# Issuing the last V tile whole and ahead of the FFN weights, with a semaphore for each weight, in a one-core decode block

## The chip, the cores and the metric

The kernel runs on one core of a Trainium2 chip. The metric is the device time of one execution in microseconds. Of the kernel before, three runs gave 677.16, 677.44 and 677.42 us (median 677.42). Every run told here was of the state "fast". The profiled execution is a little shorter by its own account (the span of the profile of before is 675.6 us), so spans are compared with spans and times with times.

## The reference

One decoding step of a transformer block: layer norm, attention of 2 x 32 heads over a cache of 8192 keys, output projection, residual, layer norm, a gated FFN, residual. Batch 2, width 512, head width 128, FFN width 1376, all bfloat16.

```python
x = A_x                                             # 2 x 1 x 512
h = x + _A_ref(_layernorm(x), A_k_cache, A_v_cache, A_wq, A_wo)
h2 = h + _B_ref(_layernorm(h), B_W_gate, B_W_up, B_W_down)
# _A_ref: q = x @ wq;  p = softmax(q k^T / sqrt(128));  (p v) @ wo
# _B_ref: (relu(x @ W_gate) * (x @ W_up)) @ W_down
```

The two caches are 268 MB, so almost all the work is to stream them through once.

## The kernel before

The 64 heads are worked off as 32 tiles p of two heads. For each p one K tile and one V tile of 4096 KB are loaded into four slots (K of even p in slot 0, V of odd p in slot 3). VectorE (DVE) computes three quarters of the scores of a K tile, TensorE (PE) the rest; ScalarE (ACT) takes the exponentials; PE multiplies them with V (128 matmuls, "the PV"). The FFN weights go to slot 0 once K30 is done with. All loads are issued by one queue, in program order:

```python
                def load_v(p, parts=None):
                    sv = (2 * p + 1) % 4
                    if p >= 2:
                        sp.wait(t_pv[p - 2])          # the slot's last reader
                    ...                               # (cut) whole, or in `parts` with sem_vl each
                # in the loop over p, after the scores of tile p:
                    if p + 2 < NP:
                        sp.wait(*t_kfree[p])
                        t_k[p + 2] = load(s, slot[s][:], kv(A_k_cache, p + 2))
                    ...                               # (cut)
                    elif p == NP - 2:                 # p = 30
                        sp.wait(*t_kfree[p])          # slot 0 free: DVE has read K30
                        for k, w in enumerate((B_W_up, B_W_gate)):
                            nc.sync.dma_start(..., w...).then_inc(sem_w, 16)
                        load_v(p + 1, vparts)         # V31 in four parts
                        nc.sync.dma_start(..., B_W_down[0:10 * 128]...).then_inc(sem_wd, 16)
```

The tail behind the loop, in PE's order (cut):

```python
                pv(NP - 2)
                t_O[3] = normalize(3, 24, 31, t_batch[3], False)   # DVE, queued behind the last scores
                pe.wait(t_O[3])
                o_proj(range(HM, 30), 0, 2)
                o_proj(range(30, 32), 0, 1)
                normalize(4, 31, 32, z_sum(4, 31, 32), True)
                pv(NP - 1)                                         # "the last PV"
                ...                                                # scale, o_proj, residual, mean
                pe.wait((sem_w, 32), t_d)
                t_u = ffn_in(Sp[1], wup, 0, FC)                    # up: 44 matmuls
                t_g = (ffn_in(Op[1], wgt, 0, FH), ffn_in(Wp, wgt, FH, FC))   # gate: 24 + 20
                ...
                pe.wait((sem_wd, 32))                              # down: 44 matmuls, then the result
```

The softmax here doesn't subtract the row's maximum and nothing guards it: scores larger than these inputs give would overflow.

## Time and profile before

| | before |
|---|---|
| time, median of 3 | 677.42 us |
| profiled span | 675.6 us |
| DMA | 281.97 MB, 417 GB/s mean |
| busy share of PE, DVE, ACT | 44%, 73%, 30% |

The page of the kernel before: the DMA rows of the 40 slices (tenths busy, and GB/s), and the chain that ended last, by engine.

```profile
DMA  9999999999999999999999999999999999999993
GB/s 373 433 434 370 430 426 432 427 430 428 434 427 430 430 434 429 432 434 427 424 428 430 431 432 434 429 432 430 426 429 428 431 428 433 428 430 392 418 411 117
...
DMA 73%; DVE 24%; PE 1%; issue 1%; SPq 0%; DVEq 0%
```

The DMA engines are busy until the last slice (16.9 us). A change to the order of the last loads can only move that last slice and a little before it.

The timeline of before, from 636 us to the end. Columns: start, duration, engine, line, operation, out<-in, count, and in brackets the idle time before it and what ended it. SPq lines are loads being issued.

```profile
638.40 0.33 SPq L428 DMA_DIRECT2D slot<-in_B_W_up_dram  x1
...
639.26 2.04 SPq L353 DMA_DIRECT2D slot<-in_A_v_cache_dram  x4
...
641.34 0.44 SPq L432 DMA_DIRECT2D slot<-in_B_W_down_dram  x1
...
658.96 1.23 PE L309 MATMUL W<-O_sb,X 128*128 128x2 bf16 x32 [6.68 <-DVE O_sb L297]
...
660.47 2.27 PE L334 MATMUL O<-e,slot 128*128 128x2 bf16 x80
...
664.30 1.44 PE L334 MATMUL O<-e,slot 128*128 128x2 bf16 x48 [1.55 <-DMA slot<-in_A_v_cache_dram]
...
667.36 1.53 PE L473 MATMUL S<-d_b,slot 128*128 128x2 bf16 x44 [0.35 <-DVE d_b L458]
...
670.19 1.47 PE L515 MATMUL O<-hd,slot 128*128 128x2 bf16 x40
```

V31 is issued only at 639.26, behind W_up and W_gate, since the queue first waits for slot 0. The last PV does 80 of its matmuls and then stands 1.55 us until another part of V31 is there. This is the one DMA wait of the tail's PE work.

The landings of before, from the view of DMA issues between 625 and 676 us (size of one, time from issue to landing). An issue's start plus this time is its landing.

```profile
slot<-in_A_v_cache_dram SPq DMA_DIRECT2D x1, 1536.0 KB, 21.5
slot<-in_B_W_up_dram SPq DMA_DIRECT2D x1, 1376.0 KB, 9.8
slot<-in_B_W_gate_dram SPq DMA_DIRECT2D x1, 1376.0 KB, 16.4
slot<-in_A_v_cache_dram SPq DMA_DIRECT2D x1, 1280.0 KB, 24.1
slot<-in_B_W_down_dram SPq DMA_DIRECT2D x1, 1280.0 KB, 26.9
```

The V31 part of 1280 KB was the third issued, at 640.20 by the chain of waits, so it landed at 664.25, which is the end of the PE wait. W_down landed at 641.34 + 26.9 = 668.2, before PE asks for it at 670.19.

### The profile page before, as it was taken

To read this page: it belongs to the slowest core of one execution; us is meant where nothing else is said; L and a number is where in the kernel's file an instruction comes from. 1 tells how busy PE (TensorE), PEld (TensorE's weight loads), DVE (VectorE), ACT (ScalarE), POOL (GpSimd) and SP (SyncE) were. 2 spreads that over 40 slices of the span, in tenths; PEclk is the share of its full clock that TensorE was granted. 3 is DMA by queue.
4 is the path that set the end of the run, shared out by engine and by line. 5 is a ranking of instruction groups with operands and counts; after the bars stand their busy time and mean duration, and the time that the engine had idled before them with its cause. 6 is when DMAs were issued, how large, how long until landed. Compare 5 with 4: busy or idle time off the path is not lost.

```text
span 675.6 us, 14430 instructions
## 1 busy us (share of the span) xinstructions
PE 294.0 (44%) x6596; PEld 266.2 (39%) x6596; DVE 493.6 (73%) x428; ACT 202.0 (30%) x523; POOL 1.7 (0%) x11
## 2 busy tenths in 40 slices
PE   2552254344445424443533444353344644334446
PEld 2442244333434423443433444343344534334335
DVE  1774577788777768877767887776788767778891
ACT  0630322233333223333312333331233332223330
POOL 1000000000000000000000000000000000000000
PEclk9955655566655566556556556555556555556555
DMA  9999999999999999999999999999999999999993
GB/s 373 433 434 370 430 426 432 427 430 428 434 427 430 430 434 429 432 434 427 424 428 430 431 432 434 429 432 430 426 429 428 431 428 433 428 430 392 418 411 117
DMA packets 15936, 281.97 MB, mean 417 GB/s; under 512 B 1442, under 2 KB 6916, under 8 KB 7044
## 3 DMA queue, kind: packets, MB, share of 16 engines
q1 hardware_dynamic: 15872, 281.06, 97.9%
q8 instruction: 51, 0.84, 0.5%
q14 instruction: 9, 0.07, 0.0%
q10 hardware_dynamic: 4, 0.00, 0.0%
HBM read 281.05 MB, written 0.00 MB: 416 GB/s over the span
## 4 chain that ended last, share of the span: by engine, by line
DMA 73%; DVE 24%; PE 1%; issue 1%; SPq 0%; DVEq 0%
DMA slot<-in_A_k_cache_dram 69%; DVE prod L366 15%; DVE tb L374 5%; DMA slot<-in_A_v_cache_dram 4%; DVE prod L374 3%; DVE scores L381 1%; PE S L473 0%; PE O L515 0%; PE O L334 0%; SPq L353 0%; SPq L135 0%; SPq L428 0%; PE W L473 0%; PE O L473 0%; PE W L309 0%
## 5 line engine op out<-in xcount | busy, mean ns | idle before, releaser
L366 DVE TENSOR_TENSOR prod<-slot,q_b 128x6144 bf16<-128x6144 bf16 x64 | 214.9, 3358 | 132.3 <-DMA slot<-in_A_k_cache_dram 131.1
L334 PE MATMUL O<-e,slot 128*128 128x2 bf16 x4096 | 118.7, 165 | 239.2 <-DMA slot<-in_A_v_cache_dram 119.8
L334 PEld LDWEIGHTS O<-e,slot 128*128 128x128 bf16 x4096 | 114.6, 104 | 243.5 <-ACT e L267 122.0
L397 ACT ACTIVATE kT<-T 128x1024 bf16<-128x1024 bf16 x128 | 126.5, 1022 | 170.6 <-PE T L391 169.7
L391 PE MATMUL T<-ident,slot 128*128 128x128 bf16 x1024 | 122.6, 306 | 77.5 <-DMA slot<-in_A_k_cache_dram 75.2
L374 DVE TENSOR_TENSOR tb<-prod 128x3072 bf16<-128x3072 bf16 (+1 forms) x128 | 148.2, 1158 | 4.4
L391 PEld LDWEIGHTS T<-ident,slot 128*128 128x128 bf16 x1024 | 99.7, 141 | 80.5 <-DMA slot<-in_A_k_cache_dram 78.2
L267 ACT ACTIVATE e<-scores 64x48 bf16<-64x48 f32 x128 | 32.8, 256 | 253.2 <-DVE scores L381 251.6
L374 DVE TENSOR_TENSOR prod<-tb 128x1536 bf16<-128x1536 bf16 (+1 forms) x128 | 84.2, 658 | 4.4
L259 PE MATMUL S<-qT,kT 128*128 128x2 bf16 x1024 | 48.2, 168 | 39.0 <-ACT kT L397 37.8
L259 PEld LDWEIGHTS S<-qT,kT 128*128 128x128 bf16 x1024 | 40.8, 107 | 57.6 <-ACT kT L397 57.6
L381 DVE TENSOR_REDUCE scores<-prod 128x48 f32<-128x384 bf16 x64 | 35.4, 553 | 2.2
L267 ACT ACTIVATION_READ_ACCUMULATOR e<-scores 64x1 f32 x128 | 23.6, 185 | 0.0
L267 ACT ACTIVATE e<-S 64x32 bf16<-64x32 f32 x64 | 12.9, 202 | 15.0 <-PE S L259 14.2
L267 ACT ACTIVATION_READ_ACCUMULATOR e<-S 64x1 f32 x64 | 12.9, 201 | 0.7
L212 DVE CAST qT<-W 128x64 bf16<-128x64 f32 x1 | 0.2, 225 | 12.0 <-PE W L207 12.0
L241 ACT ACTIVATE q_b<-O 128x512 bf16<-128x512 f32 x8 | 4.3, 595 | 15.6 <-PE O L236 15.6
L309 PE MATMUL W<-O_sb,X 128*128 128x2 bf16 (+1 forms) x136 | 5.0, 172 | 7.0 <-DVE O_sb L297 7.0
L309 PEld LDWEIGHTS W<-O_sb,X 128*128 128x128 bf16 x136 | 4.8, 118 | 7.2 <-DVE O_sb L297 7.2
L207 PE MATMUL W<-xlT,X 128*128 128x2 bf16 x128 | 3.6, 165 | 8.6 <-DMA X<-in_A_wq_dram 8.6
L207 PEld LDWEIGHTS W<-xlT,X 128*128 128x128 bf16 x128 | 3.5, 104 | 8.7 <-DMA X<-in_A_wq_dram 8.7
L285 DVE TENSOR_REDUCE zr<-O 128x16 f32<-128x48 f32 (+1 forms) x4 | 0.8, 204 | 8.3 <-PE O L277 8.3
(58 smaller groups left out, 39.3 us busy)
## 6 DMA issues: line engine op xcount, KB each, us to landing
slot<-in_A_k_cache_dram SPq DMA_DIRECT2D x32, 4096.0 KB, 27.8
slot<-in_A_v_cache_dram SPq DMA_DIRECT2D x31, 4096.0 KB, 32.2
X<-in_A_wq_dram SPq DMA_DIRECT2D x1, 4096.0 KB, 12.4
X<-in_A_wo_dram SPq DMA_DIRECT2D x1, 4096.0 KB, 49.1
slot<-in_A_v_cache_dram SPq DMA_DIRECT2D x1, 1536.0 KB, 21.5
slot<-in_B_W_up_dram SPq DMA_DIRECT2D x1, 1376.0 KB, 9.8
slot<-in_B_W_gate_dram SPq DMA_DIRECT2D x1, 1376.0 KB, 16.4
slot<-in_A_v_cache_dram SPq DMA_DIRECT2D x1, 1280.0 KB, 24.1
```

The lines of the kernel that those rows point to most:

```text
L207: i = nc.tensor.matmul(Wp[:, h * B:(h + 1) * B], lhsT=wq[:, c, h * Dh:(h + 1) * Dh], rhs=lT[:, c * B:(c + 1) * B], start=(c == 0), stop=(c ...
L241: t_cp[m] = act.run(nc.scalar.activation(out=q_b[:, m * 512:(m + 1) * 512], in_=Op[m % 2][:], func=ACT.Copy))
L259: i = nc.tensor.matmul(Sp[p % 2][:, 2 * jj:2 * jj + 2], lhsT=kT[n % 3][:, k * 128:(k + 1) * 128], rhs=qT[:, 2 * p:2 * p + 2], start=True, ...
L267: t = act.run(nc.scalar.activation(out=e_t[p % 2][q, j0:j0 + nj, a], in_=src(q, a), func=ACT.Exp, scale=inv_sqrt_dh, accum_out=zs[q, 2 * p ...
L285: dve.run(nc.vector.tensor_reduce(out=zr[:, 2 * p0:2 * p1], in_=zbank(k)[:, 64:64 + n * (NCH + 1)].rearrange("p (n k) -> p n k", k=NCH + 1 ...
L309: i = nc.tensor.matmul(Wp[:, c * B + b0:c * B + b1], lhsT=wo_m[:, h, c, :], rhs=Ov[:, h // 2, h % 2, b0:b1], start=first[0], stop=last, sk ...
L334: i = nc.tensor.matmul(Op[k % 2][:, col:col + 2], lhsT=v_t[:, j, :], rhs=e_t[p % 2][:, j, :], start=(nmm == 0), stop=(nmm == J - 1))
L366: t_dm = dve.run(nc.vector.tensor_tensor(out=prod[:], in0=k_t[:, c * JC:(c + 1) * JC, :], in1=qv, op=ALU.mult))
L374: dve.run(nc.vector.tensor_tensor(out=o, in0=cur[:, :, 0:half], in1=cur[:, :, half:w], op=ALU.add))
L381: t_s = dve.run(nc.vector.tensor_reduce(out=sc[:], in_=cur, axis=AX.X, op=ALU.add))
L391: i = nc.tensor.transpose(Tp[n % 3][:, k * 128:(k + 1) * 128], k_t[:, j, :], ident[:])
L397: t_ev[n] = act.run(nc.scalar.activation(out=kT[n % 3][:], in_=Tp[n % 3][:], func=ACT.Copy))
```

## The change

The intent: V31 needs only slot 3, so it need not wait for slot 0. The order becomes K30, K31, V30, V31, W_up, W_gate, W_down. V31 goes whole. Since the weights are now the last to land, each gets its own semaphore, and W_down comes in two parts, so that PE can start on what is there.

```diff
-        sem_x, sem_wq, sem_wo, sem_w, sem_wd, sem_out = ...
-        sem_vl = [S(f"vl{i}") for i in range(4)]
+        sem_w = [S(f"w{i}") for i in range(2)]
+        sem_wd = [S(f"wd{i}") for i in range(3)]
 ... (cut)
                     elif p == NP - 2:
+                        load_v(p + 1)
                         sp.wait(*t_kfree[p])
                         for k, w in enumerate((B_W_up, B_W_gate)):
-                            nc.sync.dma_start(...).then_inc(sem_w, 16)
-                        load_v(p + 1, vparts)
-                        nc.sync.dma_start(... B_W_down[0:10 * 128] ...).then_inc(sem_wd, 16)
+                            nc.sync.dma_start(...).then_inc(sem_w[k], 16)
+                        for k, (r0, r1) in enumerate(WD_PARTS):      # (0, 6), (6, 10)
+                            nc.sync.dma_start(... B_W_down[r0 * 128:r1 * 128] ...).then_inc(sem_wd[k], 16)
 ... (cut)
-                pe.wait((sem_w, 32), t_d)
+                pe.wait(t_d)
+                pe.wait((sem_w[0], 16))
                 t_u = ffn_in(Sp[1], wup, 0, FC)
+                pe.wait((sem_w[1], 16))
                 t_g = (...)
 ... (cut)
-                pe.wait((sem_wd, 32))
+                pe.wait((sem_wd[2], 16))
                 for k, (f0, f1) in enumerate(((0, FH), (FH, FC))):
-                    pe.wait(t_hd[k])
+                    pe.wait(t_hd[k], (sem_wd[k], 16))
```

The arithmetic of PE, DVE and ACT, and its order on each engine, does not change.

More of the change, by code (lines that the diff above doesn't have):

```diff
@@ L68, in bass_sequential_preLN__gqa_block_cached__glu_gated_reglu__decode_kernel @@
     inv_sqrt_dh = 1.0 / math.sqrt(Dh)
-    BATCH = 8
+    WD_PARTS = ((0, 6), (6, 10))
     with ExitStack() as es:
@@ L87, in bass_sequential_preLN__gqa_block_cached__glu_gated_reglu__decode_kernel @@
         slot_cnt = [0] * 4
-        sem_x, sem_wq, sem_wo, sem_w, sem_wd, sem_out = S("x"), S("wq"), S("wo"), S("w"), S("wd"), S("out")
-        sem_vl = [S(f"vl{i}") for i in range(4)]
+        sem_x, sem_wq, sem_wo, sem_out = S("x"), S("wq"), S("wo"), S("out")
+        sem_w = [S(f"w{i}") for i in range(2)]
+        sem_wd = [S(f"wd{i}") for i in range(3)]
         slot = [sb(f"slot{i}", [128, SLOT], BF16) for i in range(4)]
@@ L156, in _ @@
                 t_v[1] = load(3, slot[3][:], kv(A_v_cache, 1))
-                nc.sync.dma_start(wd_last[:], B_W_down[F - FR:]).then_inc(sem_wd, 16)
+                nc.sync.dma_start(wd_last[:], B_W_down[F - FR:]).then_inc(sem_wd[2], 16)
                 pool.run(nc.gpsimd.memset(ident_f[:], 0.0))
@@ L317, in _ @@
                 t_batch = {}
-                vparts = ((0, 96, 128), (1, 0, 48), (2, 48, 88), (2, 88, 96))
                 W_AT = 24
@@ L325, in pv @@
                     col = 2 * (p - batches[k][0])
-                    parts = vparts if p == NP - 1 else (
-                        [(0, NCH * JC, J)] + [(1 + c, c * JC, (c + 1) * JC) for c in range(NCH)])
+                    parts = [(0, NCH * JC, J)] + [(1 + c, c * JC, (c + 1) * JC) for c in range(NCH)]
                     if p == batches[k][0] and k >= 2:
@@ L330, in pv @@
                     nmm = 0
-                    for ci, (ei, j0, j1) in enumerate(parts):
-                        pe.wait(t_exp[p][ei], (sem_vl[ci], 16) if p == NP - 1 else t_v[p])
+                    for ei, j0, j1 in parts:
+                        pe.wait(t_exp[p][ei], t_v[p])
                         for j in range(j0, j1):
@@ L342, in pv, with load_v @@
                             t_O[k] = normalize(k, *batches[k], t_batch[k], False)
-                def load_v(p, parts=None):
+                def load_v(p):
                     sv = (2 * p + 1) % 4
@@ L347, in load_v @@
                         sp.wait(t_pv[p - 2])
-                    if parts is None:
-                        t_v[p] = load(sv, slot[sv][:], kv(A_v_cache, p))
-                        return
-                    src = kv(A_v_cache, p)
-                    for ci, (_, j0, j1) in enumerate(parts):
-                        nc.sync.dma_start(
-                            slot[sv][:, j0 * Dh:j1 * Dh], src[:, j0 * Dh:j1 * Dh]).then_inc(sem_vl[ci], 16)
+                    t_v[p] = load(sv, slot[sv][:], kv(A_v_cache, p))
                 for p in range(NP):
@@ L429, in _ @@
                                 slot[0][:, k * DC * F:(k + 1) * DC * F],
-                                w.rearrange("(p c) n -> p (c n)", c=DC)).then_inc(sem_w, 16)
-                        load_v(p + 1, vparts)
-                        nc.sync.dma_start(
-                            slot[0][:, 2 * DC * F:2 * DC * F + 10 * D].rearrange("p (r n) -> p r n", n=D),
-                            B_W_down[0:10 * 128].rearrange("(r p) n -> p r n", p=128)).then_inc(sem_wd, 16)
+                                w.rearrange("(p c) n -> p (c n)", c=DC)).then_inc(sem_w[k], 16)
+                        for k, (r0, r1) in enumerate(WD_PARTS):
+                            nc.sync.dma_start(
+                                slot[0][:, 2 * DC * F + r0 * D:2 * DC * F + r1 * D].rearrange("p (r n) -> p r n", n=D),
+                                B_W_down[r0 * 128:r1 * 128].rearrange("(r p) n -> p r n", p=128)).then_inc(sem_wd[k], 16)
                 pv(NP - 2)
```

## The prediction

> What bounds the kernel now. The page says DMA moves 281.97 MB at a mean 417 GB/s, and its 40 slices show DMA at tenths 9 until the last slice. A 4096 KB K or V tile takes 9.7 us of that stream. The chain of waits is 73% DMA and 24% VectorE (DVE). So the body is bound by the bytes, which stay; only the tail can change.
>
> The tail, from the timeline and the chain (us from the start of the span):
> - 627.25 K30 has landed; DVE works without a gap on tiles 30 and 31 (K31 is there by 637) until 658.3; the exponentials end at 659.0.
> - TensorE (PE) stands idle from 652 to 658.95, waiting for O_sb, which DVE normalises only behind the last scores. Then 32 output-projection matmuls, the sum, and 80 of the last PV's matmuls (from 660.47, 2.27 us).
> - At 662.74 PE waits 1.55 us for a part of V31. V31 was issued in four parts at 639.3 to 640.8, behind W_up and W_gate, as the queue first waited for slot 0 (held until 638.4).
> - 664.30 the last 48 PV matmuls (1.44 us), 665.85 scale, projection, residual, mean; 667.36 up, gate, then down at 670.19, result written, end 675.6. W_down landed at 668.2 (26.9 us after issue) and ended no wait.
>
> What the change does.
> 1. V31 waits only for PV of 29, which ended at 625.5. It is issued about 13 us earlier, ahead of the weights. [...](K30, K31, V30, up, gate, V31, down land in issue order). V30 lands at 647.0, so V31 should land at about 656.7, or 658 with an instruction fetch in the way (one of 1.0 us was served at 653.1). PE asks for it at 660.47. The wait goes.
> 2. The same bytes now end with the weights. My estimate from the trace's rates: up lands at 661.3, gate 664.5, down part 1 at 666.7, part 2 at 668.1 (its 1 KB packets take 46 ns each, 22 GB/s per engine against 27 for the large ones, as before).
> 3. The last PV runs 128 matmuls in one go, 660.47 to 664.05. Everything behind it moves up 1.6 to 1.7 us: up asked for at 665.7, gate 667.2, down part 1 at 668.5, part 2 at 669.4. All have landed by then, with 1.3 to 4 us to spare, so the separate semaphores are worth about nothing.
> 4. Three DMA issues fewer and larger V packets: off the chain.
>
> So the gain is one wait, 1.6 us; not more, since the tail then hangs on DVE's 31 us from K30's landing and the chain behind it. Predicted 675.8 us, 0.2% less; 8 times in 10 between 674.4 and 677.2. Faster by over 2%: 1%; within 2%: 98%; slower by over 2%: 1%.
>
> What would show it: no PE wait on V before the last 48 PV matmuls; the last PV still starting near 660.5; V31 issued near 626; K30 and K31 landing unchanged; hardly any PE wait on the FFN weights; span near 674.0.
>
> What would make it wrong: the last landing moves to the back of the chain. The slower eight of the 16 DMA engines land 4.7 us behind the faster eight, one of them 1.8 us behind those; part 2 of W_down could land after 669.4 and give back up to 1 us. If V31's early issue delays K30 or K31, DVE shifts and the time grows by as much.

What the trace of before shows is the order of landings in the brackets, with last landings at 627.25, 636.95, 647.03, 648.25, 655.15, 657.49 to 664.93 (V31's parts) and 668.27 us. 677.4 less the one wait of 1.6 us is the predicted 675.8 us. V31's 656.7 is V30's 647.0 plus the 9.7 us of a tile.

The other figures of the DMA are from the same trace. The packets of 1 KB took 46 ns in the median, those of 32 KB 1.215 us, which are 22 and 27 GB/s; 16 times 27 is 432 GB/s, and the page's slices show up to 434. The packet of kind "instruction" at 653.08 took 1.00 us. Of the 16 landings of W_down eight came at 661.6 to 661.9, six at 666.4 to 666.9 and two at 668.0 and 668.3; of V31's third part eight at 657.2 to 657.5, seven at 662.4 to 662.9 and one at 664.25. That a landing stands for one engine is the reading, since the trace does not number the engines.

## The result

| | before | after |
|---|---|---|
| time, median of 4 each | 677.43 us (677.16 to 677.45) | 676.11 us (675.81 to 676.30) |
| profiled span | 675.6 us | 674.2 us |

The ratio is 0.9982, with a 95% interval of 0.9968 to 0.9996. Here and below a ratio is the mean time of one kernel's fast runs over that of the other's fast runs of the same rounds, so not quite the ratio of the medians quoted. The gain is 1.3 us, 0.2%.

The page of the changed kernel: the DMA row and the chain by engine.

```profile
DMA  9999999999999999999999999999999999999993
...
DMA 70%; DVE 27%; PE 2%; issue 1%; SPq 0%; DVEq 0%
```

The last V landing is off the chain, and the last two tiles' DVE work is on it.

The timeline of the changed kernel, from 624 us to the end, in the same columns.

```profile
625.32 0.33 SPq L136 DMA_DIRECT2D slot<-in_A_v_cache_dram  x1
...
638.14 0.33 SPq L422 DMA_DIRECT2D slot<-in_B_W_up_dram  x1
...
638.98 13.50 SPq L426 DMA_DIRECT2D slot<-in_B_W_down_dram  x2
...
658.69 1.23 PE L310 MATMUL W<-O_sb,X 128*128 128x2 bf16 x32 [6.68 <-DVE O_sb L298]
...
660.21 3.55 PE L333 MATMUL O<-e,slot 128*128 128x2 bf16 x128
...
665.29 0.50 PE L467 MATMUL S<-d_b,slot 128*128 128x2 bf16 x13 [0.26 <-DVE d_b L452]
...
666.22 1.18 PE L467 MATMUL S<-d_b,slot 128*128 128x2 bf16 x31 [0.42 <-issue]
...
668.70 1.48 PE L511 MATMUL O<-hd,slot 128*128 128x2 bf16 x40
```

V31 is issued 14 us earlier and the last PV runs its 128 matmuls in one go. But there is a new stop: after 13 matmuls of up PE stands for 0.42 us, and the profile gives "issue", that is, no wait on a semaphore that it can see. W_up had landed 4 us before. (The 13.50 us of the W_down line are the queue's time on its two issues; the second began at 639.46.)

The landings of the changed kernel, from the view of DMA issues between 625 and 676 us.

```profile
slot<-in_A_v_cache_dram SPq DMA_DIRECT2D x1, 4096.0 KB, 32.4
slot<-in_B_W_up_dram SPq DMA_DIRECT2D x1, 1376.0 KB, 22.9
slot<-in_B_W_gate_dram SPq DMA_DIRECT2D x1, 1376.0 KB, 25.8
slot<-in_B_W_down_dram SPq DMA_DIRECT2D x1, 768.0 KB, 27.3
slot<-in_B_W_down_dram SPq DMA_DIRECT2D x1, 512.0 KB, 28.2
```

V31 is there at 625.3 + 32.4 = 657.7, up at 661.0, gate at 664.3, down at 666.3 and 667.7. PE asks for them at 660.2, 665.3, 667.2, 668.7 and about 669.4. No landing ends a PE wait.

Each of these is the last of 16 landings, which come in two halves: of W_down's second part eight at 660.0 to 660.8 and eight at 665.9 to 667.7, two of these at 667.4 and 667.7. The faster half is done 6.8 us before the last landing. No run here tries to even this out.

Where the 1.4 us between the two profiled spans went, stretch by stretch (differences of the starts above):

| stretch | before | after | difference |
|---|---|---|---|
| up to the start of the last PV | 660.47 | 660.21 | -0.26 |
| the last PV | 5.27 | 3.55 | -1.72 |
| scale to start of up | 1.62 | 1.53 | -0.09 |
| up and gate, to start of down | 2.83 | 3.41 | +0.58 |
| down to the end | 5.4 | 5.5 | +0.1 |

The first line is not of the change: K30's landing starts it (DVE begins on K30 at 627.27 before and 627.01 after), and this lay between 627.0 and 627.6 in the traces of all runs. So the removed wait gave 1.7 us, and a third of that was lost again in the FFN. The stop costs more than its 0.42 us of idle time: idle time counts from the modelled end of the last matmul, and the starts on its two sides are 0.59 us apart, where they are 0.03 us apart in the rest of up.

### The profile page after: what moved, and what is told of

The parts are those of the page before. It is cut to its first block, busy times and chain, and to the rows that moved or that the text cites. A ratio compares the mean times of both kernels' runs of the same rounds, so it can differ in the third digit from the quotient of the medians.

```text
span 674.2 us, 14429 instructions
## 1 busy us (share of the span) xinstructions
PE 294.7 (44%) x6596; PEld 266.7 (40%) x6596; DVE 493.6 (73%) x428; ACT 202.2 (30%) x523; POOL 1.7 (0%) x11
## 4 chain that ended last, share of the span: by engine, by line
DMA 70%; DVE 27%; PE 2%; issue 1%; SPq 0%; DVEq 0%
DMA slot<-in_A_k_cache_dram 70%; DVE prod L359 16%; DVE tb L367 6%; DVE prod L367 4%; DVE scores L374 2%; PE O L333 1%; PE S L467 0%; PE W L310 0%; PE O L511 0%; SPq L136 0%; PE W L467 0%; PE O L467 0%; PE S L278 0%; SPq L152 0%; DVE O_sb L298 0%
```

## The experiments

The theory: the gain is V31's place in the queue and nothing else; the new stop in up is a refill of PE's instructions, which the wait on V31 had hidden before. The rivals: the gain comes from the separate semaphores, or from the whole transfer with fewer issues; and the stop is chance, or belongs to its place in the program.

The record behind the second part of the theory is in the trace of DMA packets. Besides the data queue it has packets of 16 KB on a queue of kind "instruction". The page of the changed kernel counts them:

```profile
q8 instruction: 51, 0.84, 0.5%
```

PE has 13,238 records (weight loads, matmuls and sequencer instructions) in this trace, 259.6 for each of the 51 packets; the other engines have 1,191 together. The page does not say which engine a packet is for. That these packets bring PE's instructions, 256 with each (13,238 is 51.7 times 256), was the assumption when the first expectations were written; the stops found in the tails of the runs below do lie 256 records apart (12,738, 12,994 and 13,250). Whether such a packet can stop PE is what the next runs test.

All experiments gave correct results. There were twelve runs of ten kernels, in three calls on three different chips; the runs of before beside them had medians of 677.10, 677.32 and 677.48 us. Numbers of different calls are compared by their distance from before.

### a_again and a_third: the changed kernel twice more

No edit. For a_again:

> The changed kernel once more, to narrow the interval and to see whether its new 0.4 us PE stop inside the W_up matmuls comes again. Both theories: 1.2 to 1.6 us faster than before (about 676.0). If the stop is an instruction refill of PE (a 256-instruction boundary), it stands at the same matmul, the 14th weight load of W_up, in this profile too; if it is chance, it is gone or elsewhere.

For a_third:

> The changed kernel a third time, beside its padded twin. 676.0 to 676.6; PE stops 0.4 to 0.7 us at the 14th weight load of W_up again.

Measured: 676.48 us (676.27 to 676.89), ratio 0.9991 (0.9979 to 1.0004), and 676.50 us (675.98 to 676.82), ratio 0.9985 (0.9973 to 0.9998). The gain by the medians is 0.6 and 1.0 us. The stop came again at the same matmul and was longer, 0.60 us in a_again and 0.84 us in a_third. The timeline of a_third:

```profile
665.52 0.51 PE L467 MATMUL S<-d_b,slot 128*128 128x2 bf16 x13 [0.26 <-DVE d_b L452]
666.87 1.18 PE L467 MATMUL S<-d_b,slot 128*128 128x2 bf16 x31 [0.84 <-issue]
```

So it is not chance. In the three profiled executions the span grows with the stop: 674.2, 674.7 and 675.0 us with stops of 0.42, 0.60 and 0.84 us (the starts around them are 0.59, 0.76 and 1.00 us apart). The medians do not follow it: a_third has the longer stop and the larger gain. So why the gain varies between 0.6 and 1.3 us stays open. The interval of a_again includes 1; that of a_third does not.

### order_only: the new order with the old semaphores

```diff
# against the changed kernel
-    WD_PARTS = ((0, 6), (6, 10))
+    WD_PARTS = ((0, 10),)
# sem_w and sem_wd are one semaphore each again
-                pe.wait(t_d)
-                pe.wait((sem_w[0], 16))
+                pe.wait((sem_w, 32), t_d)
-                pe.wait((sem_w[1], 16))
-                pe.wait((sem_wd[2], 16))
+                pe.wait((sem_wd, 32))
-                    pe.wait(t_hd[k], (sem_wd[k], 16))
+                    pe.wait(t_hd[k])
```

> The new order and the whole V31 with the old semaphores (one for up and gate, one for W_down, which is one transfer again). My theory, that the gain is V31 standing ahead of the weights: the same time as the changed kernel within 0.3 us (about 676.0). Rival, that the gain needs the separate semaphores (up can start before gate and down land): about 677.4, no gain.

Measured: 676.58 us, ratio 0.9990 (0.9977 to 1.0004), beside 676.48 us of a_again. The order alone does what the whole change does; the rival "semaphores" fails its first test. By time alone this would be weak, since both intervals include 1. The trace is clear: V31 is issued at 625.40, the last PV runs its 128 matmuls in one go from 660.49, and PE stops 0.36 us behind the 13th matmul of up.

### sems_only: the old order with the new semaphores

```diff
# against the kernel before: V31 stays in four parts behind up and gate
-                                w...).then_inc(sem_w, 16)
+                                w...).then_inc(sem_w[k], 16)
# W_down in two parts, sem_wd[k] each; PE's waits as in the changed kernel
```

> The old order with V31 in four parts behind up and gate, and the new semaphores and the two parts of W_down. My theory: no gain, 677.4 within 0.3 us, and the wait of about 1.5 us on V31 before the last 48 PV matmuls stays. Rival, semaphores: about 676.0.

Measured: 677.08 us, ratio 0.9999 (0.9987 to 1.0012): no gain. The timeline of this run shows the V31 wait in its old place, and up without a stop:

```profile
664.07 1.44 PE L336 MATMUL O<-e,slot 128*128 128x2 bf16 x48 [1.24 <-DMA slot<-in_A_v_cache_dram]
...
667.05 1.55 PE L476 MATMUL S<-d_b,slot 128*128 128x2 bf16 x44 [0.26 <-DVE d_b L461]
```

### whole_behind: V31 whole, but behind up and gate

```diff
# against the changed kernel
-                        load_v(p + 1)
                         sp.wait(*t_kfree[p])
                         for k, w in enumerate((B_W_up, B_W_gate)):
                             nc.sync.dma_start(...).then_inc(sem_w[k], 16)
+                        load_v(p + 1)
```

> The changed kernel, but with the whole V31 issued behind up and gate, as before's parts were. My theory (place in the queue is what counts): V31 lands whole at about 664.9, the last PV starts only then instead of at 660.3, so about 2.5 us slower than before (about 679.8). Rival (the whole transfer with fewer issues is itself the gain): 677.1 or less.

Measured: 679.92 us, ratio 1.0039 (1.0026 to 1.0053). The timeline of this run:

```profile
639.05 0.42 SPq L136 DMA_DIRECT2D slot<-in_A_v_cache_dram  x1
...
664.52 3.58 PE L333 MATMUL O<-e,slot 128*128 128x2 bf16 x128 [4.12 <-DMA slot<-in_A_v_cache_dram]
```

In the old place the whole transfer costs 2.6 us, because no matmul can start before all of V31 is there. The four parts of the kernel before were the right thing for the old place.

### parts_ahead: only the place is moved

```diff
# against the kernel before
+                        load_v(p + 1, vparts)
                         sp.wait(*t_kfree[p])
                         for k, w in enumerate((B_W_up, B_W_gate)):
                             nc.sync.dma_start(...).then_inc(sem_w, 16)
-                        load_v(p + 1, vparts)
```

> The kernel before with one move: the four V31 parts are issued ahead of up and gate; old semaphores. My theory: the same time as the changed kernel, 0.6 to 1.2 us below before, no wait on V31 in the last PV. Rival (whole transfer counts): no gain.

Measured: 676.31 us, ratio 0.9984 (0.9972 to 0.9997). No V31 wait, and PE stops 0.38 us behind the 13th matmul of up, as in the changed kernel. The timeline of this run:

```profile
625.75 1.79 SPq L353 DMA_DIRECT2D slot<-in_A_v_cache_dram  x4
...
660.64 3.55 PE L334 MATMUL O<-e,slot 128*128 128x2 bf16 x128
...
665.82 0.48 PE L473 MATMUL S<-d_b,slot 128*128 128x2 bf16 x13 [0.35 <-DVE d_b L458]
...
666.68 1.18 PE L473 MATMUL S<-d_b,slot 128*128 128x2 bf16 x31 [0.38 <-issue]
```

Moving one line gives the gain of the whole change. With sems_only and whole_behind this settles the first part: the place in the queue is the cause.

### pad32, pad64, pad64_again: the instruction stream shifted

```diff
# against the changed kernel; 64 in place of 32 for pad64 and pad64_again
-                pe.wait((sem_wq, 16), t_xlT)
+                pe.wait(t_xlT)
+                for _ in range(32):
+                    nc.tensor.matmul(Op[0][:, 0:B], lhsT=ident[:], rhs=lT[:, 0:B], start=True, stop=True)
+                pe.wait((sem_wq, 16))
```

The dummy matmuls run while PE waits for wq (8.62 us in the trace of before), into a bank that is written over later. They only move everything behind them in PE's program.

> The changed kernel with 32 dummy matmuls (64 PE instructions) while PE waits for wq at the start, a pure shift of the instruction stream. If the 0.42 us stop in the W_up matmuls is a refill at a 256-instruction boundary, the boundary moves about 32 matmuls earlier, into the last PV: the stop at the 14th weight load goes or shrinks, and the time is up to 0.4 us below the changed kernel of this call (about 675.7). If it is something of that place (data, semaphore), the stop stays at the 14th weight load and the time does not change.

Measured: 676.86 us, ratio 0.9995 (0.9983 to 1.0008). The stop in up is gone, but this is a miss in time: beside a_again's 676.48 it is slower, not faster. The stop moved 31 matmuls back, about as far as the padding moves the boundary, and grew. The timeline of pad32:

```profile
660.26 3.39 PE L336 MATMUL O<-e,slot 128*128 128x2 bf16 x122
665.03 0.30 PE L336 MATMUL O<-e,slot 128*128 128x2 bf16 x6 [1.38 <-issue]
...
666.86 1.55 PE L470 MATMUL S<-d_b,slot 128*128 128x2 bf16 x44 [0.26 <-DVE d_b L455]
```

Its place was foreseen, its length was not. To see why it grew, the 16 KB packets are set beside PE's records. PE's weight loads, matmuls and semaphore instructions are numbered in order of time. The stop is at record 12,995 in the changed kernel, in its repeats, in order_only, parts_ahead and pad32. (12,995 is the first weight load behind the stop; the matmul 12,994 starts with it, within 2 ns.) Record 12,739 is 256 earlier, and pad64 below stops there; I take it as the boundary before.

```
                 record 12,739   16 KB packet      record 12,995
                 starts          read from, to     starts           stop before it
before           661.17          664.11, 665.13    667.72           no
after            660.90          663.71, 664.74    666.22           0.42
a_third          661.13          664.32, 665.39    666.87           0.84
pad32            659.70          662.46, 663.56    665.03           1.38
whole_behind     665.24          665.79, 666.78    670.00           no
```

Where PE stopped, it went on 5.3 to 5.7 us after passing record 12,739, and 1.5 us after the packet was read (1.3 to 1.6 us over all stops of this kind in the tails of all runs). PE itself needs only 3.6 us for 128 weight loads and 128 matmuls in one go (3.55 us for the last PV after). If the dependent steps between the PV and up lie between the two records, PE takes longer from one to the other and the stop is short (after, 0.42 us); if it is all PV, the stop is long (pad32, 1.38 us). Before, the V31 wait lay between the same two records: PE came to record 12,995 after 6.55 us and did not stop. This is where 0.6 to 1.0 us of the expected gain went (the distance of the starts around the stop, less 0.03).

The count holds beyond this one place. Every PE stop in the tail of any run that the profile gives as "issue" lies within a record of 12,738, 12,994 or 13,250, which are 256 apart. The kernel before has one such stop as well, in its body: 2.3 us at 532.36, at record 10,178, which is 11 x 256 before 12,994. PE went on there 1.3 us after a packet had been read, and the stop is not on the chain that ended last. All ten traces without padding have this stop (2.0 to 2.5 us), the four with padding do not.

So a stop of this kind is found in the timeline as PE idle time ended by "issue" on a matmul line (weight-load lines have other idle time under that name), always at the same count of PE's records (12,995 from the start, to within one, in four kernels and two repeats here), or a multiple of 256 from it; instructions put in ahead move other work onto that count. Such stops are few: with 51 packets, the profile of before shows PE idle by "issue" at one place, that of the changed kernel at two. Where PE stopped in the tail of any run, for 0.2 to 1.6 us, it went on 4.7 to 5.7 us after passing the boundary before.

With these times the next step could be computed instead of guessed:

> The changed kernel with 64 dummy matmuls at the start. From the traces so far: PE passes a 256-instruction boundary, the refill is read about 2.8 us later, and the block after it is usable about 5.4 us after the passing. With 32 dummies the boundary fell 0 to 2 us behind the start of PV 31 and PE stopped 1.4 us at its 123rd weight load. With 64 the boundary passed last before PV 31 lies in PE's long idle time and the next in the middle of PV 31 (about the 90th matmul, no stop), the one after in the second half of gate, 5.4 us later. Expected: no stop over 0.2 us in the tail, and a time about 0.5 us below the changed kernel, 1.2 to 1.7 us below before. If the stop stays or only wanders with the same length, the refill theory's timing is wrong.

> The padded twin (64 dummy matmuls at the start) on the same chip: 0.3 to 0.6 us below the changed kernel of this call, no stop in the tail after 655. If the two are within 0.15 us, the stop isn't worth in time what it shows in the profile.

Measured: pad64 675.98 us, ratio 0.9978 (0.9965 to 0.9992); pad64_again 675.86 us, ratio 0.9977 (0.9964 to 0.9991). Beside pad64_again, the changed kernel (a_third) took 676.50 us: 0.64 us by the medians and 0.50 by the means, though the ranges overlap (675.68 to 676.23 against 675.98 to 676.82). The timeline of pad64:

```profile
648.59 3.50 PE L336 MATMUL O<-e,slot 128*128 128x2 bf16 x126
653.36 0.19 PE L336 MATMUL O<-e,slot 128*128 128x2 bf16 x2 [1.27 <-issue]
...
660.83 3.55 PE L336 MATMUL O<-e,slot 128*128 128x2 bf16 x128
...
665.92 1.55 PE L470 MATMUL S<-d_b,slot 128*128 128x2 bf16 x44 [0.26 <-DVE d_b L455]
```

The stop now comes at record 12,739, two matmuls short of the end of the PV of 30. There PE has 5 us to spare, and it costs nothing. In pad64_again a stop of 0.19 us was left in gate, 512 records behind this one; otherwise the tail ran through.

### before_pad64: the same padding in the kernel before

The edit is that of pad64, made to the kernel before.

> The kernel before with the same 64 dummy matmuls. Before has no refill stop in its tail (PE reached the boundary 1.2 us after the block was there, held up by the V31 wait), so padding should gain nothing: the same as before within 0.3 us. If it is faster by 0.5 us too, padding gains by another way than the stop.

Measured: 677.43 us, ratio 0.9999 (0.9987 to 1.0012). The V31 wait stays (1.61 us), up runs without a refill stop, and a stop of 1.10 us stands at the end of the PV of 30, as in pad64. Padding by itself gains nothing; it gains only where the V31 wait no longer covers the refill. (The 1.2 us of the expectation are an estimate from the table: in before the packet was read to 665.13, PE goes on 1.3 to 1.6 us after a packet, and it came to record 12,995 at 667.72, 1.0 to 1.3 us after that.)

### pv_early_parts: a version to beat both

```diff
# against the changed kernel
# V31 ahead of the weights, in three parts with a semaphore each
-                        load_v(p + 1)
+                        sp.wait(t_pv[p - 1])
+                        for ci, (j0, j1) in enumerate(((NCH * JC, J), (0, JC), (JC, NCH * JC))):
+                            nc.sync.dma_start(slot[3][:, j0 * Dh:j1 * Dh], ...).then_inc(sem_vl[ci], 16)
# PE: 80 of the last PV's matmuls before the wait for O_sb, the projection behind the PV
                 t_O[3] = normalize(3, 24, 31, t_batch[3], False)
-                pe.wait(t_O[3])
-                o_proj(range(HM, 30), 0, 2)
-                o_proj(range(30, 32), 0, 1)
+                pv(NP - 1, (0, 1))
                 normalize(4, 31, 32, z_sum(4, 31, 32), True)
-                pv(NP - 1)
+                pv(NP - 1, (2,))
                 dve.wait(t_pv[NP - 1])
                 t = o_scale(4, 31, 32)
+                pe.wait(t_O[3])
+                o_proj(range(HM, 30), 0, 2)
+                o_proj(range(30, 32), 0, 1)
```

> A version meant to beat both: V31 ahead of the weights in three parts with a semaphore each, and two thirds of the last PV put on PE before the wait for O_sb, where PE idles from 652 to 658.7; the 32 projection matmuls go behind the PV and overlap the scaling on DVE. Expected: up asked for at 663.1, gate's landing (664.3) and W_down's (666.3 and 667.7) now end waits; span end about 672.2, about 3 us below before (about 674.0). If PE refills stop it, less.

Measured: 674.43 us (674.08 to 674.93), ratio 0.9956 (0.9944 to 0.9969), 2.9 us below before. The timeline of this run:

```profile
651.84 1.78 PE L334 MATMUL O<-e,slot 128*128 128x2 bf16 x59
655.15 0.72 PE L334 MATMUL O<-e,slot 128*128 128x2 bf16 x21 [1.52 <-issue]
...
662.83 1.55 PE L474 MATMUL S<-d_b,slot 128*128 128x2 bf16 x44 [0.26 <-DVE d_b L459]
...
666.69 0.93 PE L518 MATMUL O<-hd,slot 128*128 128x2 bf16 x24 [0.58 <-DMA slot<-in_B_W_down_dram]
667.98 0.66 PE L518 MATMUL O<-hd,slot 128*128 128x2 bf16 x16 [0.35 <-DMA slot<-in_B_W_down_dram]
```

The refill stop (1.52 us) falls into time in which PE has nothing else to do (it idles 2.98 us more behind that part). Now the landings of W_down, 666.6 and 667.8, end PE's waits: the tail is bound by the bytes again.

### early_waits_joined: the same version without separate waits

```diff
# against pv_early_parts
-                pe.wait((sem_w[0], 16))
+                pe.wait((sem_w[0], 16), (sem_w[1], 16))
-                pe.wait((sem_w[1], 16))
-                pe.wait((sem_wd[2], 16))
+                pe.wait((sem_wd[2], 16), (sem_wd[0], 16), (sem_wd[1], 16))
-                    pe.wait(t_hd[k], (sem_wd[k], 16))
+                    pe.wait(t_hd[k])
```

> The version with the early PV, its waits joined: up waits for up and gate, down for all of W_down. There the landings bound the end: gate lands at 664.3 and up is asked for at 662.8; down part 1 landed at 666.6, part 2 at 667.9. Expected: up starts 1.4 us later, but down still ends no earlier than part 2's landing plus 1.5 us, so about 0.5 to 0.9 us slower than the version with separate waits (about 675.2). If it is the same time, separate waits are worth nothing there either.

Measured: 675.41 us, ratio 0.9970 (0.9957 to 0.9982), against 0.9956 with separate waits on another chip: about 0.9 us by the ratios, and the ranges (675.28 to 675.49 against 674.08 to 674.93) do not meet. The timeline of this run:

```profile
664.60 1.52 PE L474 MATMUL S<-d_b,slot 128*128 128x2 bf16 x44 [1.84 <-DMA slot<-in_B_W_gate_dram]
...
668.08 1.47 PE L517 MATMUL O<-hd,slot 128*128 128x2 bf16 x40 [0.52 <-DVE r L510]
```

Up now waits 1.84 us for gate, and down for all of W_down. The second line's "DVE r" is not what it waited for: PE's program has no wait on that reciprocal before down, and part 2 of W_down landed at 667.8. So the semaphores of the change are of use, but only in a kernel that gets to the weights before they land.

## Why the prediction was right

The time, 676.11 us, lies in the predicted 674.4 to 677.2, and the mechanism was shown. The range is wide: a gain of half the predicted size would have lain in it too, so it is the traces that confirm the prediction. There is some luck in how near the first measurement came to 675.8: in its profile, K30's earlier landing (0.26 us) paid for part of what the FFN lost (0.58 us).

- *What bounds it.* Right: the body is unchanged (418 GB/s mean, after 417), and K30 and K31 landed as before within 0.3 us.
- *Step 1, V31 earlier and its wait gone.* Right: issued at 625.32 (predicted 625.5), landed at 657.7 (predicted 656.7 to 658), no wait on V31 in the last PV, which started at 660.21 (predicted near 660.5). parts_ahead shows that this move alone makes the gain; sems_only and whole_behind, that the other parts of the change make none without it.
- *Step 2, the landings of the weights.* Right within 0.4 us: predicted 661.3, 664.5, 666.7, 668.1; measured 661.0, 664.3, 666.3, 667.7.
- *Step 3, "Everything behind it moves up 1.6 to 1.7 us".* Right as far as up (2.1 us in the profile, of which 0.3 us is K30's earlier landing), not behind it. Down was asked for at 668.70, not 668.5, although up began 0.4 us earlier than predicted. The term of the sum that was mis-sized is the stretch of up and gate: it was taken over from before at 2.83 us and took 3.41. The missing time is the stop, read here as PE's instruction refill, 0.6 us in this profile and up to 1.0 us in a_third. The prediction knew such a packet, but only as something that might delay V31's landing.
- *Separate semaphores "worth about nothing".* Right for this kernel (order_only and sems_only), and early_waits_joined shows the limit of that sentence: about 0.9 us where the landings bind.
- *Step 4, fewer issues and larger packets off the chain.* Consistent (V31's packets were 32 KB in the trace of after, 2 to 12 KB in that of before): parts_ahead, with the old four parts and issues, gained 1.0 us over before, where the changed kernel gained 0.6 to 1.3 us.
- *"So the gain is one wait, 1.6 us".* The measured gain was 1.3, 0.6 and 1.0 us. With the stop moved out of the way (pad64, pad64_again) it was 1.3 and 1.6 us.

Two things stay open. That the stop is a refill is inferred from the count of 256 records and from the 16 KB packets, read 1.3 to 1.6 us before PE goes on; no run took the stop away, it could only be moved. And the packet was read 2.8 to 3.2 us after the passing in four rows of the table but 0.55 us after it in whole_behind, where most data had landed by then, and 4.1 us after it at the stop in the body of before. That suggests that it queues behind data packets, but this was not tested.

## What to carry to other kernels

Order the last loads by when each is needed and by what each must wait for: a transfer that needs slot 3 should not stand behind one that waits for slot 0. When you take a wait away, ask what it was hiding: here a stop of PE, read as a refill of its instructions, came to light (PE went on 5.3 to 5.7 us after the boundary before, and runs 256 weight loads and matmuls back to back in 3.6 us) and ate a third to over half of the removed wait. In these runs separate semaphores paid only where a landing ends a wait, so look at landing and asking times side by side before adding them.
